# Attention and feed-forward on one core: gate sum in SBUF, casts shared with GpSimd, one cast replaced by a transfer, new planner durations

## The chip, the cores and the metric

The kernel runs on one core of a Trainium2 chip. The metric is the device time of one execution in microseconds. The kernel before takes 1197.33 us, the median of 3 runs (1196.77, 1197.33 and 1201.03).

Engine names in the rows: PE is TensorE, PEld its weight loads, DVE VectorE, ACT ScalarE, POOL GpSimd, SP SyncE (whose queue, SPq, issues nearly all transfers).

## The reference

Causal attention with a decay term over 8 batches of 8 heads, 576 positions of 64 numbers each; its output, laid out as 4608 tokens of 512 numbers, goes through a feed-forward layer whose gate is softplus. All in float32.

```python
scores = scale * q @ k.T                       # per batch and head
decay  = cum[:, None] - cum[None, :]           # cum = cumsum(log(clip(f)))
scores = where(causal, -1e9, scores + decay)
attn   = exp(scores - max); attn /= sum(attn) + 1e-9
x      = attn @ v                              # -> [4608, 512]
h      = x @ w_in                              # [4608, 2048]
g      = maximum(h, 0) + log1p(exp(-abs(h)))   # softplus
out    = g @ w_out                             # [4608, 512]
```

## The kernel before

To keep float32 accuracy with fast matmuls, most operands are split into a high part of type fp32r (a cast) and a low part (the operand minus its high part), and a product is the sum of two or three fp32r matmuls.

**Attention.** The first batch is computed in plain float32 in pieces (the first 107 us). From then on a head is one job. Its q and k are loaded into `raw` (q twice, in partitions 0 to 63 and 64 to 127, and k likewise, 2 transfers of 288 KB; one buffer). `prepare` makes from it the tile `T` of four planes; there are two tiles `T`, used in turn by successive heads. Plane 0 is q's high part (cast `q_hi` over 128 partitions, whose upper half `q_lo` then turns into q's low part); plane 1 holds q's high part once more in partitions 0 to 63 (`q_hi2`) and decay rows above; plane 2 is k's high part (`k_hi`); plane 3 is k's low part (`k_lo`) and decay rows. `stat_tile` computes the scores of 5 row tiles (lines 931 and 932, two matmuls each, tile `s` in PSUM), takes the row extreme on VectorE (L936) and the exponential on ScalarE (L964, into `p`). `turn_tile` scales the exponentials into a first and a second half-precision part (L1012 on ScalarE or L1014 on GpSimd, then L1017 on VectorE, tile `cross`), a DMA transpose turns them (L1028), and `output` multiplies with v (L1199, tile `o` in PSUM) and brings the result to `x` in two steps: ScalarE (L1219), then VectorE (L1223), which ends the use of the PSUM bank. After the first batch, scores and outputs share two PSUM banks (tag `att`).

**Feed-forward.** Tokens go in blocks of 512 (the first ones shorter). For each of 16 slices of 128 hidden units, 12 matmuls at L1342 make `h` in PSUM (two banks, tag `h`); `gate` takes it through absolute value, exponential and logarithm on ScalarE (L1375, L1378, L1381, tile `e` in SBUF), then VectorE adds max(h, 0) at L1389 and writes the sum back to `h` in PSUM; then come the high part `gh` (a cast, on ScalarE or VectorE) and the low part `gl` (L1397, VectorE); then 12 matmuls at L1418 add into the output accumulators. A block can start when the attention of its tokens is done; the last 196 us hold feed-forward alone.

**The order.** A planner in the kernel places every operation once: each carries a modelled duration, the operations it follows, and the buffers it takes. It repeatedly picks the operation that can start first and appends it to its engine's instruction stream, so that each engine then runs its stream in that order and waits at each instruction for what it needs. Where an operation may run on several engines, the planner takes the one with the smallest sum of start, duration and bias. SyncE's queue is ordered in the same way: a transfer waits at the head of the queue until what it reads is ready, and those behind it wait too. Casts all stand at line 232 (a helper).

The planner's choices among engines before and after, from the built programs:

| operation | ScalarE | VectorE | GpSimd | SyncE |
|---|---|---|---|---|
| casts of q and k over 128 partitions | 73, then 61 | 39, then 6 | 0, then 45 | |
| q's second high part, 64 partitions | 38, then 0 | 18, then 0 | 0 | 0, then 56 transfers |
| cast of the gate (`gh`) | 117, then 126 | 19, then 4 | 0, then 6 | |
| high part of v | 50, then 27 | 6, then 8 | 0, then 21 | |

Of the kernel before, what the change touches and what calls it, by code (L numbers as in the profile page):

```python
# [25 lines left out]
PELAG, GLAG, PORTLAG = 0.1, 0.2, 0.09  # L26
SCALE_BIAS = 1.0
COPY_BIAS = 0.1
WINDOW = 700
RATE = 262  # L30
PLAIN = 0
# [152 lines left out]
def on_act(n, more=0.0, psum=False):  # L184
    return On("ACT", (0.067 if psum else 0.095) + n / 1200 + more)


def on_dve(n, fast=False, port=False, bias=0.0):
    return On("DVE", 0.071 + n / (1920 if fast else 960), bias, fast or port)


def on_dma(kb, n=1, eng="SP"):

    return On(eng, max(0.6 * n, kb / RATE) if eng == "SP" else 1.5 * n)
# [19 lines left out]
def copies(n):  # L214

    return [on_act(n), on_dve(n, True, bias=COPY_BIAS)]


def scales(n):
# [16 lines left out]
def tile_decay_attention_softplus_ffn(  # L236
# [62 lines left out]
    def back(box, key):  # L299
        return lambda: box[key, "back"]()  # L300
# [372 lines left out]
    def peak(b, h):  # L673

        box = {}

        def load(e):
            box["v"] = buf("vpk", [P, 2, NCH * D], f"vp{b}_{h}")
            e.dma_start(
                out=box["v"].rearrange("p h (c d) -> p h c d", c=NCH),  # L680
                in_=vR[b, h - 1 : h + 1].rearrange("h p c d -> p h c d"),
            )

        def reduce(e):
            e.tensor_reduce(
                peaks[b % 2][:, h - 1 : h + 1], box["v"], AX.X, ALU.max, apply_absolute_value=True,
            )

        if h % 2 == 0:
            return  # L690
        ld = add_dma(load, 320, takes=("vpk",))
        r = add(on_dve(2 * NCH * D), reduce, after=[ld] + peak_ops.get(b - 2, [])[-1:])
        give("vpk", [r])
        peak_ops.setdefault(b, []).append(r)
        if h < H - 1:
            return

        def store(e):
            e.dma_start(out=v_d[b].rearrange("(p h) -> p h", p=P), in_=peaks[b % 2])

        def spread(e):
            box["all"] = buf("fe", [P, 512], f"vs{b}").bitcast(BF16)[:, 0 : P * H]
            x = v_d[b]
            e.dma_start(out=box["all"], in_=bass.AP(x.tensor, x.offset, [[0, P], [1, P * H]]))

        def top(e):
            x = box["all"].rearrange("p (k h) -> p h k", h=H)
            e.tensor_reduce(v_down[b % 2], x, AX.X, ALU.max)

        def scales_(e):  # L710
            u, d = v_up[b % 2], v_down[b % 2]
            e.tensor_scalar(d, d, 2.0**-97, None, ALU.max)
            bits = 0x7F800000
            e.tensor_scalar(u.bitcast(U32), d.bitcast(U32), bits, bits, ALU.bitwise_and, ALU.bitwise_xor)
            e.tensor_scalar(d.bitcast(U32), d.bitcast(U32), bits, None, ALU.bitwise_and)
            e.tensor_scalar(u, u, 2.0**13, None, ALU.mult)
            e.tensor_scalar(d, d, 2.0**-29, None, ALU.mult)

        o = add_dma(store, 2, after=peak_ops[b])
        peak_ops[b].append(o)  # L720
        o = add_dma(spread, 256, after=[o], takes=("fe",))
        o = add(On("DVE", 1.2), top, after=[o] + scale_used.get(b - 2, []))
        give("fe", [o])
        scale_set[b] = add(On("DVE", 0.45), scales_, after=[o])

# [9 lines left out]
    def attention(job):  # L735
# [31 lines left out]
        st = {}  # L767
# [74 lines left out]
        def split_v():  # L842
            up = v_up[b % 2][:, heads[0] : heads[0] + 1]

            def v_hi(e):
                st["v16"] = buf("vhl", [P, nv, 2 * D], f"v16_{n}", F16)
                x = st["v16"][:, :, 0:D]
                if hasattr(e, "activation"):
                    e.activation(x, st["vr"][0]["v"], AF.Copy, scale=up)
                else:  # L850
                    e.tensor_scalar(x, st["vr"][0]["v"], up, None, ALU.mult)

            def v_lo(e):
                hi, lo = st["v16"][:, :, 0:D], st["v16"][:, :, D : 2 * D]
                e.scalar_tensor_tensor(lo, st["vr"][0]["v"], up, hi, ALU.mult, ALU.subtract)

            vh = add(
                [on_act(nv * D), on_dve(nv * D, bias=COPY_BIAS)], v_hi,
                after=st["V"] + [scale_set[b]], takes=("vhl",),
            )  # L860
            vl = add(subs(nv * D), v_lo, after=[vh])
            give("vraw", [vl])
            st["V"] = [vl]

        def prepare():
            def begin(e):
                nonlocal t, tb, qA, qB, kA, kB
                t = T[number % 2]
                tb = t.bitcast(F32)
                qA, qB, kA, kB = (t[:, i, :] for i in range(4))  # L870

            def decay_rows(e):
                e.dma_start(out=tb[64:ST, 1::2, :], in_=aug_d[bh])

            def q_hi(e):
                copy(e, t[:, 0, :], st["q"])

            def q_hi2(e):
                copy(e, t[0:64, 1, :], st["q"][0:64])

            def q_lo(e):
                e.tensor_sub(t[64:P, 0, :], st["q"][64:P], tb[64:P, 0, :])

            def k_hi(e):
                copy(e, t[:, 2, :], st["k"])

            def k_lo(e):
                e.tensor_sub(t[0:64, 3, :], st["k"][0:64], tb[0:64, 2, :])

            split_v()  # L890
            if number < nplain + 2:
                set_rows(number % 2, T0_end[2 * (number % 2)] + T0_end[2 * (number % 2) + 1])
            start = add(NO_ENGINE, begin, after=T_set[number % 2], takes=("T",), lag=0.0)
            a = add_dma(decay_rows, 18, after=[start, decay_ready["rows"]])
            lo_on = On("DVE", 0.75, 0.0, True)
            q1 = add(copies(S), q_hi, after=[start, st["qk"]])
            q2 = add(lo_on, q_lo, after=[q1])
            q3 = add(copies(S), q_hi2, after=[start, st["qk"]])
            k1 = add(copies(S), k_hi, after=[start, st["qk"]])
            k2 = add(lo_on, k_lo, after=[k1])  # L900
            give("raw", [q2, q3, k2])
            st["T"] = [a, q2, q3, k2]


# [85 lines left out]
        def turn_tile(ti):  # L990
# [17 lines left out]
            for w, (to1, to2), of in todo:  # L1008

                def first_part(e, to1=to1, of=of):  # L1010
                    if hasattr(e, "activation"):
                        e.activation(to1, of, AF.Copy, scale=f_)  # L1012
                    else:
                        e.tensor_scalar(to1, of, f_, None, ALU.mult)  # L1014

                def second_part(e, to1=to1, to2=to2, of=of):
                    e.scalar_tensor_tensor(to2, of, f_, to1, ALU.mult, ALU.subtract)  # L1017

                a = add(scales(w), first_part, after=deps)
                st["split"].append(  # L1020
                    add(On("DVE", 0.09 + w / 960, 0.0, True), second_part, after=[a])
                )
            if ti < nt - 1:
                return
# [161 lines left out]
        def output(gi):  # L1186
# [37 lines left out]

            needs = last + x_taken.get(b, [])
            takes = () if b in x_taken else ("x32",)
            c = add(on_act(w, psum=True), shift, after=needs, takes=takes)
            d = add(on_dve(w), put, after=[c])
            x_taken.setdefault(b, [c])
            puts = [d]  # L1230
            wrote.setdefault(b, []).append((tok, tok + w, d))
# [28 lines left out]
    def ffn_block(i):  # L1260
# [108 lines left out]
        def gate(u):  # L1369
# [11 lines left out]
                e.activation(box["e"], box["e"], AF.Ln, bias=1.0)  # L1381

            def total(e):
                h = box["t"] = st["h", u]
                if plain:
                    o = box["g"] = buf("gh", [P, 512], f"g{i}_{u}", F32R).bitcast(F32)
                    e.scalar_tensor_tensor(o, h, 0.0, box["e"], ALU.max, ALU.add)
                    return
                e.scalar_tensor_tensor(h, h, 0.0, box["e"], ALU.max, ALU.add)  # L1389

            def hi_part(e):
                box["h"] = buf("gh", [P, 512], f"gh{i}_{u}", F32R)
                copy(e, box["h"], box["t"])

            def lo_part(e):
                box["l"] = buf("gl", [P, 512], f"gl{i}_{u}", F32R)
                e.tensor_sub(box["l"], box["t"], box["h"].bitcast(F32))  # L1397

            a = add(on_act(512, psum=True), absolute, after=st["ups"][-1:], takes=("fe",))
            a = add(on_act(512), exp, after=[a])  # L1400
            a = add(on_act(512), log, after=[a])
            a = add(on_dve(512), total, after=[a], takes=("gh",) if plain else ())
            give("fe", [a])
            if plain:
                give("h", [a], back(st, ("h", u)))
                st["g", u] = box, [a]
                return
            h_ = add([on_act(512, psum=True), on_dve(512)], hi_part, after=[a], takes=("gh",))
            l_ = add(on_dve(512), lo_part, after=[h_], takes=("gl",))
            give("h", [l_], back(st, ("h", u)))  # L1410
            st["g", u] = box, [h_, l_]

        def products(e, fc, tiles, gh, gl, first, last):
# [287 lines left out]
```

## Time and profile before

| | |
|---|---|
| profiled execution, its own time | 1197.87 us |
| its span, first to last instruction | 1196.1 us |
| mean granted TensorE clock | 0.976 |
| busy: PE, DVE, ACT, POOL | 1104.4, 895.3, 849.3, 165.5 us |
| first 100 us | plain float32 pieces |
| 100 to 300 us | attention, weight splits, first feed-forward blocks |
| 300 to 1000 us | attention with feed-forward between |
| 1000 to 1196 us | feed-forward alone |

The span is 1.8 us shorter than the execution. Busy time counts an instruction from its start to its (for matmuls modelled) end; two matmuls in a row overlap, so the number that matters on TensorE is the time in which it is not busy, 1196.1 - 1104.4 = 91.7 us, and the granted clock.

### The profile page before, as it was taken

The page shows a single profiled execution, that of the slowest core. Times are in us where ns is not written, and L with a number is a line of the kernel's source. Part 1 is how long each engine was busy: PE and PEld are TensorE (multiplying, and loading weights), DVE is VectorE, ACT ScalarE, POOL GpSimd, SP SyncE. Part 2 cuts the span into 40 slices and gives each one's busy share as a digit, 9 for nine tenths or more (in the row PEclk, how much of TensorE's full clock was granted, in tenths as well). Part 3 has the DMA queues.
Part 4 walks back from the last instruction along what each step waited for, and adds up shares of the span by engine and source line. Part 5 has one row for each costly group of instructions (what it writes and reads, how often), then busy time and mean ns, then how long its engine had stood idle before and what let it go on. Part 6 is the DMA issues. An engine that isn't in the chain of part 4 may idle for free. (4 is left out here: it accounts for less than half of the span.)

```text
span 1196.1 us, 17149 instructions
## 1 busy us (share of the span) xinstructions
PE 1104.4 (92%) x5450; PEld 853.2 (71%) x5450; DVE 895.3 (75%) x2217; ACT 849.3 (71%) x1946; POOL 165.5 (14%) x203
## 2 busy tenths in 40 slices
PE   8999877869998998999999998998989999999998
PEld 6677466657776776777776776777767777888886
DVE  7889998878788888898989887988778774223222
ACT  7888686757777787787777777876768685444443
POOL 4332211111111111111112111110111110000000
PEclk9999898979999999999999999999999999999999
DMA  8967788867787767587767756676657652211210
GB/s 253 259 181 244 188 207 195 215 147 192 159 176 165 170 169 168 144 204 171 162 161 191 179 139 153 152 188 137 137 121 189 150 105 68 88 53 40 84 53 36
DMA packets 273611, 185.28 MB, mean 155 GB/s; under 512 B 224320, under 2 KB 246112, under 8 KB 273520
## 3 DMA queue, kind: packets, MB, share of 16 engines
q1 hardware_dynamic: 273352, 184.03, 62.7%
q8 instruction: 43, 0.70, 0.3%
q14 instruction: 48, 0.39, 0.1%
q10 hardware_dynamic: 168, 0.15, 0.0%
HBM read 114.16 MB, written 14.83 MB: 108 GB/s over the span
## 5 line engine op out<-in xcount | busy, mean ns | idle before, releaser
L964 ACT ACTIVATE p<-s,negm 128x288 f32<-128x288 f32 (+7 forms) x384 | 184.1, 482 | 96.8 <-DVE negm L936 93.0
L1342 PE MATMUL h<-xh,wih 128*128 128x512 f32 (+1 forms) x576 | 229.4, 401 | 0.7 <-DVE gl L1397 0.5
L1014 POOL TENSOR_SCALAR cross<-p,rsum 128x64 f16<-128x64 f32 (+3 forms) x135 | 127.1, 957 | 740.9 <-DVE rsum L980 487.4
L1342 PE MATMUL h<-xl,wih 128*128 128x512 f32 (+1 forms) x576 | 225.4, 394 | 1.4 <-DVE xl L1294 1.3
L1418 PE MATMUL acc<-woh_dt_float32r,gh 128*128 128x512 f32 x544 | 216.7, 398 | 0.0
L1418 PE MATMUL acc<-woh_dt_float32r,gl 128*128 128x512 f32 x544 | 213.9, 393 | 1.3 <-DVE gl L1397 1.3
L1418 PE MATMUL acc<-wol_dt_float32r,gh 128*128 128x512 f32 x544 | 213.9, 393 | 0.0
L1389 DVE SCALAR_TENSOR_TENSOR h<-h,e 128x512 f32<-128x512 f32 x136 | 95.0, 698 | 141.5 <-ACT e L1381 141.1
L1017 DVE SCALAR_TENSOR_TENSOR cross<-p,rsum,cross 64x64 f16<-64x64 f32 x336 | 178.5, 561 | 10.4 <-ACT cross L1012 4.4
L931 PE MATMUL s<-T 128*64 128x64 f32 x336 | 110.2, 333 | 68.5 <-DVE x L1223 32.7
L1375 ACT ACTIVATE e<-h 128x512 f32<-128x512 f32 x144 | 85.7, 595 | 119.9 <-PE h L1342 118.1
L936 DVE CUSTOM_DVE_ANT_0 s<-s,cmask 128x288 f32<-128x288 f32 (+6 forms) x320 | 136.1, 440 | 36.2 <-PE s L932 26.3
L1342 PE MATMUL h<-xh,wl 128*128 128x512 f32 (+1 forms) x576 | 153.6, 390 | 4.3 <-DMA wl<-wil_d 4.3
L931 PEld LDWEIGHTS s<-T 128*64 128x64 f32 x336 | 62.9, 187 | 108.0 <-DVE x L1223 41.0
L1342 PEld LDWEIGHTS h<-xh,wl 128*128 128x128 f32 x576 | 108.7, 196 | 28.4 <-DMA wl<-wil_d 4.9
L1342 PEld LDWEIGHTS h<-xl,wih 128*128 128x128 f32 x576 | 112.9, 196 | 22.1 <-DVE xl L1294 3.1
L1342 PEld LDWEIGHTS h<-xh,wih 128*128 128x128 f32 x576 | 112.7, 196 | 20.2 <-DVE gl L1397 1.0
L232 ACT CAST gh<-h 128x512 fp32r<-128x512 f32 x117 | 68.6, 586 | 74.1 <-DVE h L1389 73.3
L1418 PEld LDWEIGHTS acc<-woh_dt_float32r,gl 128*128 128x128 f32 x544 | 102.9, 189 | 25.5 <-DVE gl L1397 3.0
L1418 PEld LDWEIGHTS acc<-woh_dt_float32r,gh 128*128 128x128 f32 x544 | 103.5, 190 | 18.7 <-ACT gh L232 0.6
L1418 PEld LDWEIGHTS acc<-wol_dt_float32r,gh 128*128 128x128 f32 x544 | 103.3, 190 | 17.9
L1012 ACT ACTIVATE cross<-p,rsum 128x512 f16<-128x512 f32 (+3 forms) x198 | 104.7, 567 | 14.0 <-DVE rsum L980 7.3
(125 smaller groups left out, 1688.3 us busy)
## 6 DMA issues: line engine op xcount, KB each, us to landing
wl<-wil_d SPq DMA_DIRECT2D x72, 512.0 KB
raw<-in_qkT SPq DMA_DIRECT2D x112, 288.0 KB
vr<-in_vR SPq DMA_DIRECT2D x64, 160.0 KB
vp<-in_vR SPq DMA_DIRECT2D x28, 320.0 KB
out<-ob SPq DMA_DIRECT2D x35, 256.0 KB
sto<-in_w_out SPq DMA_DIRECT2D x11, 512.0 KB
sti<-in_w_in SPq DMA_DIRECT2D x9, 512.0 KB
wil_d<-wil SPq DMA_DIRECT2D x16, 256.0 KB
```

The lines of the kernel that those rows point to most:

```text
L232: (e.tensor_copy if hasattr(e, "tensor_copy") else e.copy)(out, in_)
L931: e.matmul(o, qA[:, q0:end], kA[:, a:z], start=True, stop=False)
L936: e.tensor_tensor_reduce(out=box["o"], in0=box["o"], in1=cmask[0:n_q, right - w : right], scale=-0.125, scalar=m0 if i else 3.0e38, op0=AL ...
L964: e.activation(o, box["o"], AF.Exp, bias=m1, scale=-1.0, accum_out=acc)
L1012: e.activation(to1, of, AF.Copy, scale=f_)
L1014: e.tensor_scalar(to1, of, f_, None, ALU.mult)
L1017: e.scalar_tensor_tensor(to2, of, f_, to1, ALU.mult, ALU.subtract)
L1342: e.matmul(o, l, r, start=m == 0, stop=m == 11)
L1375: e.activation(box["e"], st["h", u], AF.Abs)
L1389: e.scalar_tensor_tensor(h, h, 0.0, box["e"], ALU.max, ALU.add)
L1418: e.matmul(st["acc", tt], l, r[fc], start=first and m == 0, stop=last and m == 2,)
```

## The change

The gate's sum is written over `e` in SBUF instead of over `h` in PSUM; the bank of `h` is given back after the sum, and the buffer of `e` only after `gl`. The casts of the gate, of q and of k may also go to GpSimd (`casts`: ScalarE, GpSimd, or VectorE with a bias of 0.5 us), and so may the high part of v. q's second high part is no cast of `raw` any more but a transfer inside `T`, from plane 0 to plane 1, issued by SyncE after `q_hi`. `raw` is free after the two subtractions. Five modelled durations are changed.

```diff
+def on_pool(n):
+    return On("POOL", 0.2 + n * 0.0018)
...
+def casts(n, more=0.0):
+    return [on_act(n, more), on_pool(n), on_dve(n, True, bias=SPARE_BIAS)]
...
-        o = add(On("DVE", 1.2), top, after=[o] + scale_used.get(b - 2, []))
+        o = add(On("DVE", 1.9), top, after=[o] + scale_used.get(b - 2, []))
...
-                [on_act(nv * D), on_dve(nv * D, bias=COPY_BIAS)], v_hi,
+                [on_act(nv * D, 0.09), on_dve(nv * D, bias=SPARE_BIAS), On("POOL", 1.07)], v_hi,
...
             def q_hi2(e):
-                copy(e, t[0:64, 1, :], st["q"][0:64])
+                e.dma_start(out=tb[0:64, 1, :], in_=tb[0:64, 0, :])
...
-            q1 = add(copies(S), q_hi, after=[start, st["qk"]])
+            q1 = add(casts(S), q_hi, after=[start, st["qk"]])
             q2 = add(lo_on, q_lo, after=[q1])
-            q3 = add(copies(S), q_hi2, after=[start, st["qk"]])
-            k1 = add(copies(S), k_hi, after=[start, st["qk"]])
+            q3 = add_dma(q_hi2, 144, after=[q1])
+            k1 = add(casts(S), k_hi, after=[start, st["qk"]])
             k2 = add(lo_on, k_lo, after=[k1])
-            give("raw", [q2, q3, k2])
+            give("raw", [q2, k2])
...
-                    add(On("DVE", 0.09 + w / 960, 0.0, True), second_part, after=[a])
+                    add(On("DVE", 0.12 + w / 960, 0.0, True), second_part, after=[a])
...
-            c = add(on_act(w, psum=True), shift, after=needs, takes=takes)
-            d = add(on_dve(w), put, after=[c])
+            c = add(on_act(w, 0.095, psum=True), shift, after=needs, takes=takes)
+            d = add(On("DVE", 0.136 + w / 960), put, after=[c])
...
-                e.scalar_tensor_tensor(h, h, 0.0, box["e"], ALU.max, ALU.add)
+                e.scalar_tensor_tensor(o, st["h", u], 0.0, box["e"], ALU.max, ALU.add)
...
-            give("fe", [a])
+            give("h", [a], back(st, ("h", u)))
...
-            h_ = add([on_act(512, psum=True), on_dve(512)], hi_part, after=[a], takes=("gh",))
-            l_ = add(on_dve(512), lo_part, after=[h_], takes=("gl",))
-            give("h", [l_], back(st, ("h", u)))
+            h_ = add(casts(512), hi_part, after=[a], takes=("gh",))
+            l_ = add(subs(512), lo_part, after=[h_], takes=("gl",))
+            give("fe", [l_])
```

The order that the planner makes of it is shown at two places. VectorE before, around the preparation of one head's `T` in the middle of the program (the casts and subtractions of `T` at lines 232, 882 and 888, the row extremes at 936, the gate at 1389 and 1397):

```order
L1397 TENSOR_TENSOR gl_3_4160<-h_3_4071,gh_3_4148 128x512
L232 CAST T_1298<-raw_4097 128x576
L936 ISA s_4_288_4172,negm_76<-s_4_288_4172,cmask,negm_76 128x288
L936 ISA negm_76 128x1
L882 TENSOR_TENSOR T_1298<-raw_4097,T_1298 64x576
L232 CAST T_1298<-raw_4097 128x576
L888 TENSOR_TENSOR T_1298<-raw_4097,T_1298 64x576
L977 SCALAR_TENSOR_TENSOR lsum_80<-lsum_80,part_84 128x5
L979 TENSOR_SCALAR lsum_80<-lsum_80 128x5
L980 RECIPROCAL rsum_88<-lsum_80 128x5
L1389 SCALAR_TENSOR_TENSOR h_4_4151<-h_4_4151,e_4_4175 128x512
```

VectorE now, at the same head (line numbers are those of the changed kernel: 894 and 900 are the two subtractions, 1399 and 1407 the gate):

```order
L1407 TENSOR_TENSOR gl_3_4162<-e_3_4117,gh_3_4150 128x512
L948 ISA s_4_288_4170,negm_76<-s_4_288_4170,cmask,negm_76 128x288
L948 ISA negm_76 128x1
L894 TENSOR_TENSOR T_1298<-raw_4081,T_1298 64x576
L900 TENSOR_TENSOR T_1298<-raw_4081,T_1298 64x576
L989 SCALAR_TENSOR_TENSOR lsum_80<-lsum_80,part_84 128x5
L991 TENSOR_SCALAR lsum_80<-lsum_80 128x5
L992 RECIPROCAL rsum_88<-lsum_80 128x5
L1399 SCALAR_TENSOR_TENSOR e_4_4173<-h_4_4153,e_4_4173 128x512
```

Both casts have left VectorE's stream (one stands on ScalarE now, one on GpSimd); the two subtractions stand next to each other, each behind a cast of another engine. SyncE's queue before, at the heads in front of it (`raw` is the load of q and k, `vr` and `vp` loads of v, `wl` feed-forward weights):

```order
L838 DMA raw_3792<-in_qkT 64x1152 x2
L1028 DMA_TRANSPOSE cross<-cross 128x30x128
L784 DMA vr_3849<-in_vR 128x320
L679 DMA vp_3_3864<-in_vR 128x2x320
L873 DMA T_1298<-aug_d 4x2x576
L1315 DMA wl_2_3908<-wil_d 128x1024
L838 DMA raw_3931<-in_qkT 64x1152 x2
```

And now:

```order
L850 DMA raw_3794<-in_qkT 64x1152 x2
L1040 DMA_TRANSPOSE cross<-cross 128x30x128
L796 DMA vr_3850<-in_vR 128x320
L885 DMA T_1298<-aug_d 4x2x576
L691 DMA vp_3_3877<-in_vR 128x2x320
L891 DMA T_1298<-T_1298 64x576
L850 DMA raw_3908<-in_qkT 64x1152 x2
```

The transfer of q's high part (L891) stands behind the decay rows and in front of the next head's load of q and k, one for each head.

## Rows read from the trace of the kernel before

**Rows 1.** Part 1 of the page: busy time, share and instructions of each engine.
```profile
PE 1104.4 (92%) x5450; PEld 853.2 (71%) x5450; DVE 895.3 (75%) x2217; ACT 849.3 (71%) x1946; POOL 165.5 (14%) x203
```

**Rows 2.** Busy time by stretch: length, engines (instructions), PEclk, DMA share, GB/s.
```profile
0.00:100.00 100.00, 94.89 (x613) 67.55 (x614) 82.43 (x228) 79.70 (x190) 32.90 (x62) 1.00 0.82 232
100.00:300.00 200.00, 162.96 (x873) 124.32 (x872) 177.86 (x456) 147.54 (x358) 34.34 (x37) 0.91 0.78 195
300.00:1000.00 700.00, 654.40 (x3137) 505.65 (x3136) 581.00 (x1459) 531.18 (x1251) 98.23 (x104) 0.98 0.69 160
1000.00:1196.00 196.00, 192.18 (x833) 155.63 (x831) 54.02 (x77) 90.84 (x150) 0.00 (x0) 1.00 0.17 57
```

**Rows 3.** TensorE's waits from 100 to 300: total us, times, longest.
```profile
PE s L931 <- DVE T L882: 11.9, 6, 4.7
PE s L931 <- ACT p L964: 5.9, 6, 2.0
PE s L931 <- ACT xh L232: 5.5, 1, 5.5
PE s L932 <- DVE T L888: 4.8, 9, 1.1
```

**Rows 4.** TensorE's waits from 300 to 1000.
```profile
PE s L931 <- DVE x L1223: 30.2, 36, 3.6
PE s L931 <- ACT p L964: 10.1, 22, 1.4
```

**Rows 5.** Groups of instructions by shape: count, busy us, mean ns, idle before.
```profile
L232 ACT CAST T<-raw 128x576 fp32r<-128x576 f32 x73 | 48.8, 669 | 5.6 <-DMA raw<-in_qkT 5.0 <-PE s L931 0.4
L232 ACT CAST T<-raw 64x576 fp32r<-64x576 f32 x38 | 25.4, 669 | 0.9 <-DMA raw<-in_qkT 0.8
L232 DVE CAST T<-raw 128x576 fp32r<-128x576 f32 x39 | 18.0, 462 | 23.5 <-DMA raw<-in_qkT 16.9 <-PE s L931 6.2
L232 DVE CAST T<-raw 64x576 fp32r<-64x576 f32 x18 | 8.1, 447 | 0.1
L232 DVE CAST gh<-h 128x512 fp32r<-128x512 f32 x19 | 13.0, 682 | 0.2
L849 ACT ACTIVATE v<-vr,v_up 128x320 f16<-128x320 f32 x50 | 27.7, 554 | 0.5 <-DVE v_up L716 0.2
L232 ACT CAST gh<-h 128x512 fp32r<-128x512 f32 x117 | 68.6, 586 | 74.1 <-DVE h L1389 73.3
L232 ACT CAST wih<-woh_dt_float 128x512 fp32r<-128x512 f32 x12 | 7.2, 617 | 0.7 <-DVE woh_dt_float L543 0.6
```

**Rows 6.** Subtractions on VectorE, the first from PSUM, the second from SBUF.
```profile
L1397 DVE TENSOR_TENSOR gl<-h,gh 128x512 fp32r<-128x512 f32 x136 | 93.3, 686 | 27.0 <-ACT gh L232 26.2
L589 DVE TENSOR_TENSOR wil<-woh_dt_float,wih 128x512 fp32r<-128x512 f32 x16 | 10.6, 682 | 0.0
```

**Rows 7.** Groups on GpSimd, by shape.
```profile
L1014 POOL TENSOR_SCALAR cross<-p,rsum 128x512 f16<-128x512 f32 x44 | 70.1, 1593 | 0.0
L535 POOL TENSOR_SCALAR wol_dt_float<-sto 128x512 uint16<-128x512 uint16 x10 | 8.5, 853 | 20.0 <-DMA sto<-in_w_out 19.6
L232 POOL COPY cross<-rsum 128x128 f32<-128x128 f32 x10 | 5.0, 499 | 30.9 <-DVE rsum L980 22.2 <-PE b L1085 8.7
```

**Rows 8.** VectorE's smallest second part (L1017), as a group by shape.
```profile
L1017 DVE SCALAR_TENSOR_TENSOR cross<-p,rsum,cross 64x64 f16<-64x64 f32 x56 | 25.4, 453 | 6.8 <-POOL cross L1014 4.1 <-ACT cross L1012 2.2
```

**Rows 9.** Line 1017 by itself: ns min/median/max, first and last start.
```profile
L1017 DVE SCALAR_TENSOR_TENSOR cross<-p,rsum,cross x336: 252/603/1116, 133.6 to 988.8; 64x64 f16<-64x64 f32 x56, 128x512 f16<-128x512 f32 x54, 128x384 f16<-128x384 f32 x31, 128x256 f16<-128x256 f32 x22
```

**Rows 10.** Timeline (start, us): one head's preparation ends, its first scores start.
```profile
586.93 0.75 DVE L888 TENSOR_TENSOR T<-raw,T 64x576 fp32r<-64x576 f32 x1
...
603.60 0.24 PE L931 MATMUL s<-T 128*64 128x64 f32 x1
```

**Rows 11.** A piece of the chain that ended last: start, us, what.
```profile
866.60 5.05 DMA raw<-in_qkT
```

**Rows 12.** Line 1028, the transpose's issue on SyncE: ns min/median/max.
```profile
L1028 SPq DMA_TRANSPOSE cross<-cross x56: 4450/4555/5317, 138.1 to 989.7; - x56
```

More of the change, by code (lines that the diff above doesn't have):

```diff
@@ L28 @@
 COPY_BIAS = 0.1
+SPARE_BIAS = 0.5
 WINDOW = 700
@@ L1383, in total @@
             def total(e):
-                h = box["t"] = st["h", u]
+                o = box["e"]
                 if plain:
                     o = box["g"] = buf("gh", [P, 512], f"g{i}_{u}", F32R).bitcast(F32)
-                    e.scalar_tensor_tensor(o, h, 0.0, box["e"], ALU.max, ALU.add)
-                    return
-                e.scalar_tensor_tensor(h, h, 0.0, box["e"], ALU.max, ALU.add)
+                e.scalar_tensor_tensor(o, st["h", u], 0.0, box["e"], ALU.max, ALU.add)
             def hi_part(e):
                 box["h"] = buf("gh", [P, 512], f"gh{i}_{u}", F32R)
-                copy(e, box["h"], box["t"])
+                copy(e, box["h"], box["e"])
             def lo_part(e):
                 box["l"] = buf("gl", [P, 512], f"gl{i}_{u}", F32R)
-                e.tensor_sub(box["l"], box["t"], box["h"].bitcast(F32))
+                e.tensor_sub(box["l"], box["e"], box["h"].bitcast(F32))
             a = add(on_act(512, psum=True), absolute, after=st["ups"][-1:], takes=("fe",))
@@ L1402, in gate @@
             a = add(on_dve(512), total, after=[a], takes=("gh",) if plain else ())
-            give("fe", [a])
+            give("h", [a], back(st, ("h", u)))
             if plain:
-                give("h", [a], back(st, ("h", u)))
+                give("fe", [a])
                 st["g", u] = box, [a]
                 return
-            h_ = add([on_act(512, psum=True), on_dve(512)], hi_part, after=[a], takes=("gh",))
-            l_ = add(on_dve(512), lo_part, after=[h_], takes=("gl",))
-            give("h", [l_], back(st, ("h", u)))
+            h_ = add(casts(512), hi_part, after=[a], takes=("gh",))
+            l_ = add(subs(512), lo_part, after=[h_], takes=("gl",))
+            give("fe", [l_])
             st["g", u] = box, [h_, l_]
```

## The prediction

> **What bounds the kernel now.** I read the busy times first, then the stretches, then TensorE's waits inside the stretches, and last the groups by shape. TensorE is busy 92% of the span, VectorE 75%, ScalarE 71%, GpSimd 14% [rows 1]. The stretches say where the missing 8% lies: 37.0 us without a matmul from 100 to 300, 45.6 us from 300 to 1000, and 9 us in the other two together [rows 2]. Nothing in the last 196 us can gain: VectorE works 54 us there, and the matmuls that stand in that stretch are the same after the change. [...]
>
> In the first attention stretch VectorE is the full engine (177.9 of 200 us), and TensorE's scores wait for the low parts of q and k: 11.9 us in 6 waits and 4.8 us in 9 [rows 3]. There the preparation of `T` is late. From 300 on it is early: the low part of k is done at 587.68, and that head's scores start at 603.60, since the two tiles `T` alternate [rows 10]. The waits there are for the PSUM banks: 30.2 us in 36 waits until VectorE has brought an output to `x`, and 10.1 us until ScalarE has read scores [rows 4]. Both are ends of queues: VectorE is busy 581 of 700 us, ScalarE 531 [rows 2], and the awaited instruction stands behind others.
>
> **The change part by part.** Work off VectorE, counts from the built programs: 33 casts of 128 partitions x 462 ns = 15.2 us, 18 of q's second part x 447 = 8.0, 15 gate casts x 682 = 10.2 [rows 5]; together 33 us. Off ScalarE: 12 + 38 casts of q and k x 669 ns = 33.5 us, 23 of v x 554 = 12.7 us; on it come 9 gate casts x 617 = 5.6 us, and each of the 117 others reads SBUF, where the same shape took 617 ns against 586 from PSUM, 3.6 us [rows 5]; net 37 us. A few scalings of `p` and two of v change engines; they sum to a few us either way and are left out.
>
> The gate's sum and low part keep their length. A subtraction of this size took 686 ns with an operand in PSUM and 682 ns with both in SBUF [rows 6]: 136 x 4 ns is half a microsecond, nothing. [...]
>
> GpSimd receives 45 casts of 576 columns, 21 of v, 6 of the gate. No such cast stands in the trace. By the column, the half-precision scaling gives 1593 x 576/512 = 1.79 us, the 16-bit one 853 x 576/512 = 0.96 us, and the small copy, fixed part included, 499 x 4.5 = 2.25 us [rows 7]. I take 1.3 us, between the first two and near the planner's own 1.24 (an estimate); the ends stay for the range. That is 45 x 1.3 = 58 us, v by the scaling 21 x 1.0 = 21, the gate 6 x 1.2 = 7: about 86 us on an engine that has 1030 us free [rows 1]. It costs something next door: the 64-column second part on VectorE takes 252 ns at best and 453 in the mean [rows 8, 9], so 56 x 201 ns = 11 us lie in waiting while GpSimd works, on 165.5 us of GpSimd work. 86 us more make it about 6 us more if in proportion (zero to 27 us, the latter if all 136 `gl` also lose 201 ns). VectorE's net relief is 33 - 6 = 27 us.
>
> [...]
>
> Now what this is worth on TensorE.
>
> (a) 100 to 300: 15 waits for the low parts, 16.7 us [rows 3]. One of three casts leaves the preparation, 669 ns at most for each wait, 10 us; none, if the transfer that takes its place lands last. I take 5.
>
> (b) 300 to 1000: about 7/9 of the relief falls here, 21 us of VectorE and 29 of ScalarE. I let the waiting behind a queue go with its busy over its idle share, which is an estimate. VectorE: from 0.83/0.17 to 0.80/0.20, 18% less of 30.2 us, 5.4. ScalarE: from 0.759/0.241 to 0.717/0.283, 19% less of 10.1, 2.0 [rows 2, 4]. Together 7.
>
> (c) The clock fell where TensorE paused. If its loss shrinks as the pauses do: 5/37 of 18 us and 7/46 of 14 us, 4.5.
>
> The gate's bank is free two instructions earlier, but TensorE hardly waits for `gl` (no row of it among the large waits), so that is 0. The truer durations for the output steps, too: they may let the planner put feed-forward where TensorE now stands, up to the rest of the 30.2 us, or nothing.
>
> Sum: 5 + 7 + 4.5 = 16.5 us off the profiled execution's 1197.9, which is 1181.4; that execution was 0.5 us above the median, so 1181.
>
> **The rivals.** *Nothing moves.* Each wait stays, because planned order and real order disagree by as much as before and only other names end the waits. For it: idle engines cost nothing, and from 300 on the casts have 16 us to spare [rows 10]. Against: VectorE is 89% busy from 100 to 300. Time 1197, give or take 6.
>
> *The order fits better.* With shorter queues and truer durations half of the waits shown go: 28.1 + 40.3 = 68.4 us, half 34 [rows 3, 4], and 34/82.6 of the clock's 32 us, 13. Time 1150. Against: a reshuffled order makes new misfits.
>
> *GpSimd's casts hold VectorE up (slower).* In the new order the two subtractions stand at the head of VectorE's queue, each behind a cast of another engine, and the sums of the exponentials stand behind them; formerly VectorE made one of the casts itself and went on. If a cast takes 2.25 us instead of the planned 1.24, each of 45 costs 1.0 us of VectorE's time, more than the 27 us relieved. The first 16 heads have 11 of these casts, and there nothing covers them: 11 us straight to TensorE; the other 34 us undo (a) and (b) and lengthen the queue waits by some 5; with the clock's share 3: about 1217. At 1.79 us it is 0.55 of that, 1208. It decides above 1.24 + 27/45 = 1.84 us a cast.
>
> *q's transfer comes late (slower).* It waits in SyncE's queue for q's cast, can stand behind a transpose that holds the queue 4.55 us [rows 12], and must still land; the double load of q and k took 5.05 us [rows 11], so 0 to 5 us. The work beside it (the second cast and two subtractions) is about 2 us. In the middle of the program 16 us cover it; where the preparation is late already, 15 times, 1.5 us each gives 22 us, less the 7 of (b) and some clock: 1210.
>
> **How the numbers follow.** Forecast 0.43, nothing 0.21, better order 0.14, GpSimd 0.13, transfer 0.09. A measurement of this kernel can tell about 0.5%, 6 us. Faster takes the forecast nearly whole (0.41) and the better order: 0.55. Same takes nothing moves and the forecast's edge: 0.22. Slower the last two and the tail of nothing moves: 0.23. The forecast's own range is 1172 to 1191 (its terms doubled or halved). The range for 8 in 10 leaves out about the farther half of the better order and of the slower two: 1161 to 1211.
>
> **What would show it.** Right: VectorE busy about 865 to 870 us, ScalarE about 812, GpSimd near 250; TensorE's pauses shrink both before and after 300, waits for the low parts by a third, waits for `x` by a fifth; PEclk in 100 to 300 above 0.91. Each step wrong: (a) if scores wait for the transfer into `T`, or the waits for the subtractions stay at 17 us; (b) if the waits for `x` stay at 30 us though VectorE is less busy; the cast if its mean is far from 1.3 us; the contention if `gl` averages well above 686 ns. The forecast fails if VectorE's idle time ahead of the two subtractions grows by more than its busy time shrinks.

## The result, and the profile after

The changed kernel takes 1168.52 us, the median of 4 runs, against 1198.28 for the kernel before (4 runs): ratio 0.9759, 95% interval 0.972 to 0.9798. The forecast was 1181, with a range of 1161 to 1211. The direction came out as predicted; the size is nearly double (29.8 us instead of 16.3).

Part 1 of the page of after, to be read against [rows 1]:

```profile
PE 1097.8 (94%) x5450; PEld 846.6 (73%) x5450; DVE 872.9 (75%) x2152; ACT 819.7 (70%) x1879; POOL 234.5 (20%) x279
```

VectorE lost 22 us of work, ScalarE 30, GpSimd took 69 more. Predicted were 865 to 870, about 812 and near 250 us of busy time; the three numbers are close. The stretches of after, with the columns of [rows 2]:

```profile
0.00:100.00 100.00, 95.01 (x610) 67.33 (x611) 81.03 (x223) 77.98 (x186) 32.94 (x62) 1.00 0.81 230
100.00:300.00 200.00, 166.16 (x884) 123.79 (x884) 179.19 (x451) 146.31 (x358) 51.31 (x53) 0.91 0.88 210
300.00:1000.00 700.00, 673.92 (x3255) 523.69 (x3254) 569.08 (x1418) 519.10 (x1213) 150.29 (x165) 1.00 0.73 171
1000.00:1166.00 166.00, 162.69 (x705) 131.80 (x703) 43.62 (x62) 76.31 (x124) 0.00 (x0) 1.00 0.16 54
```

The span went from 1196.1 to 1166.1 us, 30.0 less. Time without a matmul fell from 37.0 to 33.8 us in 100 to 300, and from 45.6 to 26.1 us in 300 to 1000: 3.2 and 19.5 us. The two ends give another 0.7. The last 6.6 us are TensorE's busy time, 1104.4 to 1097.8, for the same 5450 matmuls: the traces' records of the granted clock hold two values, 1.0 and 0.5, and those at 0.5 sum to 59.2 us before and 47.9 us after. In both traces the starts of two feed-forward matmuls in a row (128x512) lie 227 ns apart in the median at 1.0 and 427 at 0.5; by an estimate from these numbers half of the difference, 5.7 us, is the clock's. So two thirds of the gain lie in pauses after 300.

TensorE's waits after, from 300 to 960 (total us, times, longest; neither occurs again up to 1000; compare [rows 4]):

```profile
PE s L943 <- DVE x L1235: 13.2, 22, 1.5
PE s L943 <- ACT p L976: 8.1, 21, 1.5
```

The scores' wait for the output step `x` fell from 30.2 us in 36 waits to 13.2 us in 22. The wait for the exponentials fell by 2 us. In 100 to 300 the low parts of q and k, 16.7 us in [rows 3], are gone from the list, but the wait for the exponentials, 5.9 us there, grew by 9.2 us:

```profile
PE s L943 <- ACT p L976: 15.1, 14, 3.6
...
PE s L944 <- DMA T<-T: 2.1, 2, 1.2
```

The second row is q's transfer: it was late for two heads, 2.1 us in all. The groups by shape of after (count, busy us, mean ns, idle time before), to be read against [rows 5 to 8]:

```profile
L1407 DVE TENSOR_TENSOR gl<-e,gh 128x512 fp32r<-128x512 f32 x136 | 94.1, 692 | 27.3 <-ACT gh L244 26.6
L244 ACT CAST gh<-e 128x512 fp32r<-128x512 f32 x126 | 77.9, 618 | 68.3 <-DVE e L1399 67.9
L894 DVE TENSOR_TENSOR T<-raw,T 64x576 fp32r<-64x576 f32 x56 | 42.7, 763 | 5.3 <-ACT T L244 4.1
L863 POOL TENSOR_SCALAR v<-vr,v_up 128x320 f16<-128x320 f32 x21 | 38.0, 1807 | 11.7 <-PE o L1211 11.7
L244 POOL CAST T<-raw 128x576 fp32r<-128x576 f32 x45 | 33.5, 745 | 319.9 <-PE s L943 282.7 <-DMA raw<-in_qkT 23.8 <-DVE lsum L989 9.6
L1029 DVE SCALAR_TENSOR_TENSOR cross<-p,rsum,cross 64x64 f16<-64x64 f32 x56 | 26.3, 469 | 6.2 <-POOL cross L1026 3.2 <-ACT cross L1024 2.4
```

GpSimd's cast takes 745 ns, not 1.3 us, and two of VectorE's instructions are hardly longer beside GpSimd's added work: 453 became 469 ns for the 64-column second part, 686 became 692 for `gl`. VectorE's idle time ahead of the first subtraction is 5.3 us over 56 heads, so it hardly stands behind GpSimd.

**What a pause looked like.** The longest one before, 3.63 us, from the timeline of TensorE, ScalarE and VectorE (start, us; in brackets how long the engine had waited, and for what):

```profile
870.48 1.51 PE L1199 MATMUL o<-cross,v 128*128 128x64 f16 x11
871.68 0.82 DVE L232 CAST T<-raw 128x576 fp32r<-128x576 f32 x2 [3.06 <-DMA raw<-in_qkT]
871.72 0.67 ACT L232 CAST T<-raw 128x576 fp32r<-128x576 f32 x1 [1.31 <-DMA raw<-in_qkT]
872.42 0.31 ACT L1219 ACTIVATE x<-o,v_down 64x64 f32<-64x64 f32 x1
...
873.04 1.62 ACT L1012 ACTIVATE cross<-p,rsum 128x256 f16<-128x256 f32 x3 [0.31 <-DVE rsum L980]
874.13 1.11 DVE L1017 SCALAR_TENSOR_TENSOR cross<-p,rsum,cross 64x64 f16<-64x64 f32 x1 [0.34 <-POOL cross L1014]
...
875.28 0.29 DVE L1223 SCALAR_TENSOR_TENSOR x<-o,v_down,x 64x64 f32<-64x64 f32 x1
...
875.62 0.24 PE L931 MATMUL s<-T 128*64 128x64 f32 x1 [3.63 <-DVE x L1223]
```

The head's last outputs end at 871.99. The next instruction in TensorE's order is the next head's first score, which needs a bank of `att`. The bank waits for `x` on VectorE, and that stands behind a cast whose load came late, a subtraction and second parts that waited for GpSimd's first ones. After, at another head:

```profile
844.02 1.51 PE L1211 MATMUL o<-cross,v 128*128 128x64 f16 x11
...
845.27 0.29 DVE L1235 SCALAR_TENSOR_TENSOR x<-o,v_down,x 64x64 f32<-64x64 f32 x1
845.37 0.47 PE L1354 MATMUL h<-xh,wih 128*128 128x512 f32 x1
...
846.61 0.40 PE L1354 MATMUL h<-xl,wih 128*128 128x512 f32 x1
846.85 0.19 PE L943 MATMUL s<-T 128*64 128x64 f32 x1
```

Six feed-forward matmuls stand between the last output and the first score, and by the end of them `x` is long done. (In this head it was hardly late: it ended at 845.56, 0.03 us behind the outputs, so there was little to cover.) Counted over the timelines from 300 to 960: before, 24 of 42 heads start right behind an output, with 17.5 us of pauses in front of them, and 18 with feed-forward between, 1.6 us. After, 14 of 43 start right behind an output, 4.5 us, and 29 do not, 0.0 us. One row of the groups, always from 300 to 960, shows the sum of these pauses: the first score of each head, whose last column is the pause before it. Before it reads

```profile
L931 PE MATMUL s<-T 128*64 128x64 f32 x42 | 9.5, 227 | 19.1 <-DVE x L1223 17.7 <-ACT cross L1012 1.0
```

and after

```profile
L943 PE MATMUL s<-T 128*64 128x64 f32 x43 | 8.8, 204 | 4.5 <-DVE x L1235 4.5
```

14.6 of the 19.5 us lie in this row.

Feed-forward in front is not all of it. For each head, take the end of the first step of `x` (64 columns) less the end of the outputs. The positive ones sum to 36.8 us before (42 heads) and 24.0 us after (44 heads): `x` also comes sooner. Of this lateness 16.4 us before, but only 3.5 us after, falls where the next head's first score comes next in TensorE's order; the rest, 20.4 and 20.5 us, falls where other matmuls stand between.

### The profile page after: what moved, and what is told of

Its sections match the earlier page's. It is cut to its first block, busy times and chain, and to the rows that moved or that the text cites. A ratio compares the mean times of both kernels' runs of the same rounds, so it can differ in the third digit from the quotient of the medians.

```text
span 1166.1 us, 17463 instructions
## 1 busy us (share of the span) xinstructions
PE 1097.8 (94%) x5450; PEld 846.6 (73%) x5450; DVE 872.9 (75%) x2152; ACT 819.7 (70%) x1879; POOL 234.5 (20%) x279
## 4 chain that ended last, share of the span: by engine, by line
PE 51%; DVE 26%; ACT 10%; issue 6%; DMA 5%; SPq 2%; POOL 1%; DVEq 0%; POOLq 0%; ACTq 0%
PE h L1354 21%; PE acc L1428 19%; DVE cross L1029 6%; DVE s L948 3%; ACT p L976 3%; DVE x L1235 3%; PE s L943 3%; DMA raw<-in_qkT 2%; PE s L944 2%; DVE e L1399 1%; DVE gl L1407 1%; PE o L1211 1%; DVE T L894 1%; SPq L1040 1%; DVE T L900 1%
## 5 line engine op out<-in xcount | busy, mean ns | idle before, releaser
L1354 PE MATMUL h<-xl,wih 128*128 128x512 f32 (+1 forms) x576 | 222.5, 389 | 3.2 <-DVE xl L1306 3.2
L1399 DVE SCALAR_TENSOR_TENSOR e<-h,e 128x512 f32<-128x512 f32 x136 | 93.3, 686 | 141.1 <-ACT e L1393 139.5
L1029 DVE SCALAR_TENSOR_TENSOR cross<-p,rsum,cross 64x64 f16<-64x64 f32 (+2 forms) x336 | 181.5, 574 | 9.1 <-POOL cross L1026 3.6
L1026 POOL TENSOR_SCALAR cross<-p,rsum 128x512 f16<-128x512 f32 (+4 forms) x139 | 120.7, 884 | 298.9 <-DVE rsum L992 122.5
L1354 PE MATMUL h<-xh,wl 128*128 128x512 f32 (+1 forms) x576 | 150.0, 382 | 0.0
L244 ACT CAST gh<-e 128x512 fp32r<-128x512 f32 x126 | 77.9, 618 | 68.3 <-DVE e L1399 67.9
L1354 PEld LDWEIGHTS h<-xh,wl 128*128 128x128 f32 x576 | 106.0, 190 | 22.7
L1407 DVE TENSOR_TENSOR gl<-e,gh 128x512 fp32r<-128x512 f32 x136 | 94.1, 692 | 27.3 <-ACT gh L244 26.6
```

Of the source, the lines that this page charges most:

```text
L244: (e.tensor_copy if hasattr(e, "tensor_copy") else e.copy)(out, in_)
L1354: e.matmul(o, l, r, start=m == 0, stop=m == 11)
L1399: e.scalar_tensor_tensor(o, st["h", u], 0.0, box["e"], ALU.max, ALU.add)
L1407: e.tensor_sub(box["l"], box["e"], box["h"].bitcast(F32))
```

## The experiments

Two theories. *Relief*: VectorE and ScalarE have less to do, so the ends of their queues come sooner. *Order* ("truer order" in the recorded expectations): the new durations make the planner put feed-forward in front of the scores. Two expectations add a third, the *bank*: the bank of `h` comes free earlier. Four kernels do one part alone, four undo one part, four test what these left.

### One part alone

The kernel before with the new durations alone:

```diff
-        o = add(On("DVE", 1.2), top, after=[o] + scale_used.get(b - 2, []))
+        o = add(On("DVE", 1.9), top, after=[o] + scale_used.get(b - 2, []))
-                [on_act(nv * D), on_dve(nv * D, bias=COPY_BIAS)], v_hi,
+                [on_act(nv * D, 0.09), on_dve(nv * D, bias=COPY_BIAS)], v_hi,
-                    add(On("DVE", 0.09 + w / 960, 0.0, True), second_part, after=[a])
+                    add(On("DVE", 0.12 + w / 960, 0.0, True), second_part, after=[a])
-            c = add(on_act(w, psum=True), shift, after=needs, takes=takes)
-            d = add(on_dve(w), put, after=[c])
+            c = add(on_act(w, 0.095, psum=True), shift, after=needs, takes=takes)
+            d = add(On("DVE", 0.136 + w / 960), put, after=[c])
```

> The kernel before with the five new durations alone (peak reduction 1.9, second part +0.03, ScalarE's output step +0.095, VectorE's output step +0.065, v's cast +0.09); no instruction is added or removed. Relief theory (the gain comes from work taken off VectorE and ScalarE): 1192 to 1199, since no work goes. Truer-order theory (the gain comes from an order that fits the real durations): 1175 to 1188, with TensorE's waits for x from 300 to 1000 well under 30 us.

Measured: 1181.69 us, ratio 0.9841 (0.9821 to 0.9861). The instructions are the same (15 of ScalarE's 1946 went to VectorE and GpSimd, and VectorE is 6 us busier); what differs is the order, and it is worth 1.6%, as *order* had expected. Its row of first scores:

```profile
L931 PE MATMUL s<-T 128*64 128x64 f32 x43 | 8.9, 207 | 3.3 <-DVE x L1223 3.2
```

The pause went from 19.1 to 3.3 us, and 12 of 43 heads now start right behind an output. `x` is late by 30.8 us in sum, 3.0 of them with the first score next in order. This is the order theory, with VectorE and ScalarE together as busy as before (1743.7 us against 1744.6). But the row is not the whole: TensorE's time without a matmul from 300 to 960 fell only from 45.1 to 35.3 us, since pauses in front of a head's later scores grew.

The gate's sum in SBUF alone, its cast on ScalarE or VectorE:

```diff
-                e.scalar_tensor_tensor(h, h, 0.0, box["e"], ALU.max, ALU.add)
+                e.scalar_tensor_tensor(o, st["h", u], 0.0, box["e"], ALU.max, ALU.add)
...
-            h_ = add([on_act(512, psum=True), on_dve(512)], hi_part, after=[a], takes=("gh",))
+            h_ = add(copies(512), hi_part, after=[a], takes=("gh",))
```

> The kernel before with the gate's sum in SBUF alone (casts of the gate on ScalarE or VectorE). Relief theory: the instructions keep their lengths, but a cast from SBUF on VectorE can be short, so that ScalarE loses up to 50 us; 1188 to 1196. Truer-order theory: 1195 to 1201. A bank theory (TensorE gains because the bank of h comes free earlier) would give under 1185.

Measured: 1204.02 us, ratio 1.003 (1.0013 to 1.0047): no gain by itself, neither from the bank of `h` that comes free earlier nor from the 20 us less that VectorE and ScalarE have to do together (1724.1 us).

The transfer alone (q's second high part):

```diff
-                copy(e, t[0:64, 1, :], st["q"][0:64])
+                e.dma_start(out=tb[0:64, 1, :], in_=tb[0:64, 0, :])
...
-            q3 = add(copies(S), q_hi2, after=[start, st["qk"]])
+            q3 = add_dma(q_hi2, 144, after=[q1])
```

> The kernel before with q's second high part moved by a transfer alone. It takes 38 casts off ScalarE (25 us) and 18 off VectorE (8 us). Relief theory: 1185 to 1191. Truer-order theory: 1194 to 1200. If the transfer comes late: over 1200, with scores that wait for the transfer into T.

Measured: 1177.13 us, ratio 0.9799 (0.9779 to 0.9819), the best single part, and lower than either theory had expected. The row:

```profile
L931 PE MATMUL s<-T 128*64 128x64 f32 x43 | 9.7, 225 | 8.9 <-DVE x L1223 8.3 <-ACT p L964 0.3
```

Half of the pause went, though 25 of 43 heads still start right behind an output; each such pause is shorter (5.9 us over 25, against 17.5 over 24). Taking a cast per head away also gives another order, and this run does not part the two.

GpSimd allowed for the casts of q, k and v alone:

```diff
-            q1 = add(copies(S), q_hi, after=[start, st["qk"]])
+            q1 = add(casts(S), q_hi, after=[start, st["qk"]])
```

and the same for `q_hi2`, `k_hi` and v's high part.

> The kernel before with the casts of q, k and v allowed on GpSimd (gate unchanged, q's second part still a cast). Some 65 casts and 14 of v go there. Relief theory: 1183 to 1190. Truer-order theory: 1194 to 1200. GpSimd rival: slower than 1198, with VectorE waiting for GpSimd's casts.

Measured: 1196.48 us, ratio 0.9974 (0.9953 to 0.9995). Of the casts of `T`, 65 left the other two engines, and the pause before first scores stayed, at 20.8 us. (The profiled execution was a long one, 1204.77 us.) Next to nothing moved. It is a test of relief for ScalarE alone, though: ScalarE's busy time fell by 33 us, to 816.3, but VectorE's did not fall (898.8 us against 895.3).

### One part undone

The kernel after with `q_hi2` as a cast again:

```diff
-            q3 = add_dma(q_hi2, 144, after=[q1])
+            q3 = add(casts(S), q_hi2, after=[start, st["qk"]])
```

> The changed kernel with q's second high part made by a cast again (any of the three engines may take it; 37 of 56 go to GpSimd). Relief theory: GpSimd takes most of it, so little is lost, 1169 to 1175. If the transfer carries the gain: 1178 or more.

Measured: 1176.73 us, ratio to before 0.9789 (0.9751 to 0.9827). That lies between the two expectations, and its interval overlaps that of after: by the ratios a loss of 0.3%, unclear. In the profiled executions, 1176.30 against 1167.93 us, TensorE stands 8.3 us longer from 300 to 960 (34.0 us against 25.7). Alone, the same edit had gained 2.0%.

After without GpSimd's casts:

```diff
-    return [on_act(n, more), on_pool(n), on_dve(n, True, bias=SPARE_BIAS)]
+    return [on_act(n, more), on_dve(n, True, bias=COPY_BIAS)]
```

and the same for v's high part.

> The changed kernel with no casts on GpSimd: those of the gate, of q, k and v go to ScalarE or VectorE. Relief theory: VectorE takes 33 more casts of q and k and 81 of the gate, 1180 to 1188. If GpSimd's share carries nothing: 1166 to 1171.

Measured: 1189.39 us, ratio 0.9889 (0.9855 to 0.9924), close to what relief had expected: VectorE has 53 us more to do than in after (925.9 us), ScalarE 38.5 less. The pause in front of first scores stayed short, so it lies elsewhere:

```profile
L943 PE MATMUL s<-T 128*64 128x64 f32 x42 | 9.1, 216 | 4.4 <-DVE x L1235 3.5 <-DMA T<-T 0.6
```

After with the gate's sum in PSUM (the edit of the second run, reversed, one line of it shown; the gate's casts leave GpSimd with it):

```diff
-                e.scalar_tensor_tensor(o, st["h", u], 0.0, box["e"], ALU.max, ALU.add)
+                e.scalar_tensor_tensor(h, h, 0.0, box["e"], ALU.max, ALU.add)
```

> The changed kernel with the gate's sum in PSUM as before, its cast on ScalarE or VectorE. Relief theory: hardly any work moves, 1168 to 1174. Bank theory: 1178 or more.

Measured: 1185.15 us, ratio 0.9858 (0.982 to 0.9897). That is where the recorded expectation put the bank of `h`, but the trace does not show the bank: from 100 to 1000 the matmuls of `h` wait for `gl` once, 1.5 us. Here too the pause in front of first scores is as short as in after:

```profile
L943 PE MATMUL s<-T 128*64 128x64 f32 x43 | 8.8, 204 | 4.8 <-DVE x L1235 4.1 <-POOL cross L1026 0.7
```

After with four old durations:

```diff
-            c = add(on_act(w, 0.095, psum=True), shift, after=needs, takes=takes)
-            d = add(On("DVE", 0.136 + w / 960), put, after=[c])
+            c = add(on_act(w, psum=True), shift, after=needs, takes=takes)
+            d = add(on_dve(w), put, after=[c])
```

and the same for `top` and the second part; v's keeps its 0.09.

> The changed kernel with the durations of the kernel before for the peak, the second part and the two output steps. Relief theory: 1168 to 1174, as the work is the same. Truer-order theory: 1180 to 1195, with TensorE's waits for x from 300 to 1000 back near 30 us.

Measured: 1197.81 us, ratio 0.9958 (0.9933 to 0.9983): five sixths of the gain are gone. With the first run it speaks against relief. Part 1 of its page:

```profile
PE 1102.5 (93%) x5450; PEld 852.1 (72%) x5450; DVE 879.0 (74%) x2173; ACT 814.0 (68%) x1870; POOL 232.4 (20%) x267
```

VectorE and ScalarE together have 1693 us of work, as in after (872.9 + 819.7) and 52 us less than before; the relief is all there in sum, though the casts of `T` lie otherwise (VectorE makes 26 of them, 6 in after). Yet TensorE stands 45.2 us from 300 to 960 (660 less its busy time, the second number) against 25.7 in after and 45.1 before:

```profile
300.00:960.00 660.00, 614.77 (x2962) 475.88 (x2961) 543.56 (x1368) 479.22 (x1139) 146.72 (x154) 0.99 0.75 173
300.00:960.00 660.00, 634.32 (x3080) 492.05 (x3079) 555.12 (x1397) 498.85 (x1179) 150.29 (x165) 0.99 0.76 176
300.00:960.00 660.00, 614.89 (x2947) 474.80 (x2946) 555.89 (x1399) 503.04 (x1190) 94.91 (x100) 0.98 0.70 163
```

(This run, after, before.) Its row of first scores is like that of before:

```profile
L943 PE MATMUL s<-T 128*64 128x64 f32 x42 | 9.1, 217 | 21.1 <-DVE x L1235 17.1 <-POOL v L863 2.3 <-DVE lsum L989 1.6
```

27 of 42 heads start right behind an output again, with 17.5 us of pauses, and `x` is late by 36.1 us in sum, 14.8 of them with the first score next.

### What these left

How much does any other order move the time? One constant of the planner, the assumed time until VectorE's result is seen, is changed by 10 ns, in the kernel after and in the kernel before:

```diff
-SEEN = {"PE": 0.23, "ACT": 0.14, "DVE": 0.13, "POOL": 0.08, "": 0.1}
+SEEN = {"PE": 0.23, "ACT": 0.14, "DVE": 0.14, "POOL": 0.08, "": 0.1}
```

> The changed kernel with one planner constant moved that none of the parts touches: the lag that the planner allows until a result of VectorE is seen, 0.14 us for 0.13. The work stays (60, 5 and 47 casts of q and k on the three engines against 61, 6 and 45), the order shifts. If differences of 1 to 2% between the earlier variants come from the order's own scatter, this run differs from 1168.5 by 6 us or more; if they are worth their part, it stays within 4 us.

Measured: 1169.75 us, ratio 0.973 (0.9709 to 0.9751), as after. TensorE's order differs from after's in 0.3% of its matmuls, so this run says little about other orders.

> The kernel before with the same constant moved, 0.14 for 0.13, and nothing else. Scatter theory: it differs from the kernel before by 6 us or more, most likely downwards, if the kernel before was an unlucky order. Parts theory: within 4 us of it.

Measured: 1197.8 us, ratio 0.9966 (0.9951 to 0.9981). In the trace 10% of TensorE's matmuls stand elsewhere in the order, and the time differs by a third of a per cent. The pause in front of first scores halved even so:

```profile
L931 PE MATMUL s<-T 128*64 128x64 f32 x42 | 9.6, 229 | 9.2 <-DVE x L1223 8.7
```

1.6 and 2.0% are more than a third of a per cent, but those parts also change more of the order: 37% of the matmuls with the new durations, 32% with the transfer. How far a meaningless change of that size moves the time was not measured.

The two winners together, the new durations and the transfer, in the kernel before (the edits of the first and the third run):

```diff
+            q3 = add_dma(q_hi2, 144, after=[q1])
...
+            d = add(On("DVE", 0.136 + w / 960), put, after=[c])
```

> The kernel before with the durations and q's transfer, the two parts that gained alone (19 and 24 us), without the gate's move and without GpSimd's casts. If the two gains are worth their part and add: about 1159. If they end the same waits: 1172 to 1180. If each was partly a lucky order: above 1177.

Measured: 1193.93 us, ratio 0.9938 (0.9915 to 0.996). A miss: worse than either part alone, and by the recorded reading (above 1177) each of the two gains was partly a lucky order. Its row, of a profiled execution of 1200.04 us, the longest of seven:

```profile
L931 PE MATMUL s<-T 128*64 128x64 f32 x42 | 9.4, 225 | 14.7 <-DVE x L1223 14.4 <-ACT p L964 0.2
```

16 of 42 heads start right behind an output, hardly more than with the durations alone, but these pauses are long: 11.0 us over 16, against 3.3 over 12.

The kernel after with GpSimd's durations as its own trace shows them:

```diff
-    return On("POOL", 0.2 + n * 0.0018)
+    return On("POOL", 0.17 + n * 0.001)
...
-                [on_act(nv * D, 0.09), on_dve(nv * D, bias=SPARE_BIAS), On("POOL", 1.07)], v_hi,
+                [on_act(nv * D, 0.09), on_dve(nv * D, bias=SPARE_BIAS), On("POOL", 1.75)], v_hi,
```

> The changed kernel with GpSimd's durations as the trace of it shows them: a cast of 576 columns 0.75 us in the mean (planned 1.24), the high part of v 1.75 us (planned 1.07). GpSimd then gets 64 casts of q and k, 21 of the gate, 7 of v. Relief and truer-order theories both: 1158 to 1168. [...]

Measured: 1196.82 us, ratio 0.9955 (0.9939 to 0.9972). A miss again, for both theories: truer numbers cost four fifths of the gain, with VectorE and ScalarE together as busy as in after (1692.7 us against 1692.6). The planner gives GpSimd more casts (64 of `T` and 21 of the gate, 45 and 6 in after). Its cast and its first scores, 300 to 960:

```profile
L244 POOL CAST T<-raw 128x576 fp32r<-128x576 f32 x47 | 39.3, 842 | 298.4 <-PE s L943 219.5 <-DMA raw<-in_qkT 65.0 <-PE o L1211 11.3
```

```profile
L943 PE MATMUL s<-T 128*64 128x64 f32 x43 | 8.8, 205 | 14.5 <-DVE x L1235 12.5 <-DMA out<-ob 1.4 <-POOL cross L1026 0.5
```

In the same stretch of after a cast takes 737 ns. 17 of 43 heads start right behind an output, with 13.2 us. Whether more sharing with GpSimd or the order of the rest made these pauses long was not parted.

All runs side by side, each by its profiled execution (us). The fourth column is TensorE's time without a matmul from 300 to 960; the last is the part of it in front of first scores.

| run | execution | VectorE and ScalarE busy | no matmul, 300 to 960 | before first scores |
|---|---|---|---|---|
| before | 1197.87 | 1744.6 | 45.1 | 19.1 |
| before, constant changed | 1193.35 | 1739.9 | 40.2 | 9.2 |
| durations alone | 1180.68 | 1743.7 | 35.3 | 3.3 |
| gate's sum alone | 1202.24 | 1724.1 | 48.0 | 14.9 |
| transfer alone | 1178.50 | 1715.6 | 32.5 | 8.9 |
| GpSimd alone | 1204.77 | 1715.1 | 41.9 | 20.8 |
| durations and transfer | 1200.04 | 1712.4 | 41.0 | 14.7 |
| after | 1167.93 | 1692.6 | 25.7 | 4.5 |
| after, constant changed | 1169.70 | 1691.1 | 26.5 | 4.6 |
| no transfer | 1176.30 | 1725.6 | 34.0 | 3.6 |
| no GpSimd casts | 1189.81 | 1707.1 | 35.7 | 4.4 |
| gate in PSUM | 1186.58 | 1702.7 | 37.1 | 4.8 |
| old durations | 1193.30 | 1693.0 | 45.2 | 21.1 |
| GpSimd as measured | 1198.81 | 1692.7 | 43.1 | 14.5 |

The load does not order the times: three kernels with 1693 us of work lie 31 us apart. Nor does the pause in front of first scores alone: four kernels (durations alone, no transfer, no GpSimd casts, gate in PSUM) have it at 3.3 to 4.8 us, as after, and stand 8 to 11 us longer in all. By their timelines that time lies in front of a head's later scores, which wait for `x` too: 26 to 28 us against 17 in after.

## Why the prediction was right or wrong

The measured time lies in the stated range, but below 1172, where the forecast's own range ended; the lower end of the stated range was set by the rival of the better order. So the direction was foreseen for a reason that the runs bear out only in part, and part of the hit is luck.

*What bounds the kernel.* Right: TensorE's waits for `x` from 300 on were the largest thing to win, and they paid.

*(a) Low parts in 100 to 300, 5 us.* 3.2 us came. The waits for the low parts went entirely, 16.7 us, but 15.1 us of waits for the exponentials stand there now, 5.9 before. With the old durations the two low parts are waited for 17.1 us again, but VectorE makes 11 casts of `T` in this stretch there, against 1 in after, so that run does not part relief from order here. The sum of the pauses did not hang on these waits: the durations alone kept 16.5 us of them and had the smallest sum in this stretch of all runs, 29.0 us.

*(b) Shorter queues in 300 to 1000, 7 us.* 19.5 us came, and the reason given for the 7 fell. It let the waiting go with VectorE's and ScalarE's load. After with the old durations has the load of after and the pauses of before, and the durations alone gained 1.6% with the load of before. (GpSimd's casts alone gained 0.3%, but took nothing off VectorE.)

*The term counted at 0.* This, with (b), is the step that failed: the truer durations "may let the planner put feed-forward where TensorE now stands, up to the rest of the 30.2 us, or nothing". I saw the mechanism and took its lower end. Alone it gained 1.6%; without it the kernel after is 2.0% slower (0.9958 over 0.9759). The waits for `x` fell by 17.0 of 30.2 us, not by a fifth.

*(c) The clock, 4.5 us.* 5.7 us in the two profiled executions, but not where it was looked for: the granted clock stayed at 0.91 in 100 to 300 and rose from 0.98 to 1.00 behind it. The size is near by luck in part: over the whole span, the four executions of after show 0.974 to 0.980, and those of before in the later runs 0.968 to 0.979. No run shows the 18 and 14 us behind this term, nor the 32 us that the rival of the better order takes: they are 0.09 x 200 and 0.02 x 700 by the mean clock of [rows 2], and the trace of before shows 59.2 us at 0.5, half of which is 29.6.

*The costs.* The load taken off VectorE and ScalarE came out within 8 us. Two prices were off in opposite directions: GpSimd's cast 745 ns instead of 1.3 us, its scaling of v 1807 ns instead of 1.0 us, together 71.5 us instead of 79. The scaling of v was priced by the column from GpSimd's scaling of `p`; at best, 1079 ns, it is near that price, but its median is 1610 and its longest 2824, and why it spreads was not looked into. The 6 us of VectorE's time lost beside GpSimd came near: all second parts together took 3.0 us more (178.5 to 181.5) and `gl` 0.8. (In the trace of before, the 64-column second part took 252 to 275 ns where GpSimd was idle, 6 of 56, and 484 in the mean where GpSimd was busy throughout, 48 of 56.) `gl` with both operands in SBUF takes 692 ns, 6 more than with one in PSUM.

*The rivals.* GpSimd holding VectorE up fell: it decided above 1.84 us a cast, and VectorE waited 5.3 us ahead of the 56 first subtractions. That `gl` would lose as much beside GpSimd as the second part, the upper end of 27 us, is seen in sign at most: 453 to 469 ns and 686 to 692 ns beside 69 us more of GpSimd's work. The late transfer fell: two waits, 2.1 us. *The order fits better*, half of the waits shown gone and 1150, came nearest in its cause, the order, with too large a size; that the order is better because it fits is not shown. Between it and the forecast lies the measured time.

*What stays open.* The parts do not add up: alone they give 1.6, 2.0, 0.3% and a loss of 0.3%; undone from after, 2.0% (durations), 1.3% (GpSimd), 1.0% (gate) and about 0.3% (transfer, within the intervals). Each undoing also makes another order, so GpSimd's and the gate's share in after may be relief or order. Why the two winners together lose, and why truer GpSimd durations lose, was not settled; the runs only show that the pauses in front of first scores come back. Both keep the new durations, so these do not carry the gain by themselves: that the order decides is shown, that the new durations help because they are truer is not, and a lucky order is not excluded.

## What to carry to other kernels

Where a planner writes the order, an edit of its durations is an edit of the kernel: price it by asking which work will stand in front of the instruction that now waits, and how soon what it waits for will come; do not count it at zero because no instruction changes. Look for the pause that comes back once per head, and see in the timeline what stands between the end of one step and the instruction that needs its buffer. Time the parts alone and undone before crediting any of them, since effects of order do not add, and measure how far a meaningless change of order moves the time, with one that changes as much of the order as the edit does.

## What was not expected of the hardware

GpSimd's cast of 128 x 576 from float32 to fp32r, 745 ns in the mean, is not far above ScalarE's for the same shape:

```profile
L244 ACT CAST T<-raw 128x576 fp32r<-128x576 f32 x61 | 40.3, 668 | 9.3 <-DMA raw<-in_qkT 6.3 <-PE s L943 2.0 <-issue 1.0
```

The same engine needs 1807 ns in the mean, and 1079 ns at least, for v's scaling by a number per partition to half precision, on 320 columns only. A price by the column taken from one operation on GpSimd did not hold for another here: the prediction's three gave 0.96 to 2.25 us for the cast.
